# One of eight Q loads split into a half and eight small pieces, in an attention kernel that streams K and V

## The chip, the cores and the metric

The kernel runs on one core of one Trainium2 chip. The metric is the device time of that core in microseconds; lower is better. A core has a matrix engine (TensorE, PE in the profile, with its weight loads as PEld), a vector engine (DVE), a scalar engine (ACT), a general engine (POOL), and a sync engine (SP), which in this kernel issues every DMA. The DMAs of one core are carried out by 16 DMA engines side by side; a transfer adds 16 to its semaphore when it has landed.

## The reference

Grouped-query attention: 16 batches, 32 query heads over 8 key/value heads, 16 query positions, 2048 keys, head size 128, bf16.

```python
B, Hq, Hkv, Sq, Sk, D = 16, 32, 8, 16, 2048, 128
k = jnp.repeat(k, rep, axis=1)          # rep = 4
v = jnp.repeat(v, rep, axis=1)
scores = jnp.einsum("bhqd,bhkd->bhqk", q, k) * D ** -0.5
p = jax.nn.softmax(scores, axis=-1)
return jnp.einsum("bhqk,bhkd->bhqd", p, v)
```

The keys and the values are 64 MiB each; q and the result are 2 MiB each. Every key and value is used by only 64 query rows (4 heads of 16 positions).

## The kernel before, in words

There are 128 groups (batch times key/value head). Two groups make a pair, so that 64 + 64 query rows fill 128 partitions: 64 pairs, `p` from 0 to 63. K is loaded for two pairs at a time (2 MiB, 32 loads, three buffers `Kn`), V for one pair (1 MiB, 64 loads, eight buffers `Vb`; the last one in two parts, `LASTV`), Q for eight pairs (256 KiB, eight loads, numbered `c` = 0 to 7, two buffers `Qn`). The result of a pair is 32 KiB, from twelve buffers.

For a pair, DVE transposes K (`kt`, L562), PE forms the scores into PSUM (`scores`, L406 and L376), DVE copies them out negated and takes the row minimum (`negated`, L573), ACT takes the exponential (L674), PE transposes the probabilities (L414), ACT copies them back (L683), PE multiplies by V (L429, L483, L489), and ACT, or DVE for the last five, scales the result (L697, L701, L655). Q is masked into a block layout by POOL (`lay_part`, L255, four parts for each Q load), transposed by PE (`q_turn`, L392) and copied out by ACT (L664).

The order of the DMAs is written out by hand in one loop of SP (L351 to L367). At step `t` come, if their step is due: a Q load (`load_q`; for `c` of 3 and more at `t = 8c - 13`, so `c` = 7 at `t` = 43), the K load of pairs `t` and `t + 1` (even `t`), a V load (`load_v`), a result's store. SP works them off strictly in turn: each waits for the semaphore that says that its buffer is free, then is issued. A Q load waits for the POOL parts of the Q load two before it (L339).

All eight Q loads have the same form: 128 partitions, and in each partition 8 rows of 128 values, 2 KiB that lie together in HBM. Each adds 16 to the semaphore of its buffer, `sem_q[c % 2]`. POOL waits for it ahead of the first part of that load (L279); its target is 16 times the number of loads so far into that buffer.

Of the kernel before, what the change touches and what calls it, by code (L numbers as in the profile page):

```python
# [18 lines left out]
NQ = 2  # L19
# [7 lines left out]
QAHEAD = 6  # L27
LOOP = (3, 26)
QUNIT = 2
EVBASE = 4  # L30
NMBASE = 6
QTBASE = 1
# [16 lines left out]
def bass_standalone__gqa_softmax__sampling_kernel(  # L49
# [28 lines left out]
    Qn = [sb(f"Qn{i}", [128, 8, 128], BF16) for i in range(NQ)]  # L78
# [17 lines left out]

    def o_done(p):
        return sem_o[p // NOG % (NO // NOG)], 16 * NOG * (p // NO)

    scratch = Sneg[NS - 1]  # L100
    iota_t = scratch[:, 0:128].bitcast(I32)
# [12 lines left out]
    sem_q = [sem(f"sem_q{i}") for i in range(NQ)]  # L114
# [26 lines left out]
    NQP = 4 * NQC  # L141
    assert M0 >= QUNIT and M1 % 2 == 0 and M1 + QAHEAD <= NQP
    bank_used = [None] * NSTAGE

    def pe_op(*op):
        pe_prog.append(op)
# [17 lines left out]
    for p in range(2 * M1):  # L164
# [9 lines left out]
        pe_op("S", p + 2)  # L174
        if m < QUNIT:
            for k in ((4,), (5,), (6, 7), ())[p]:
# [43 lines left out]
    for op in pe_prog:  # L220
# [5 lines left out]
        elif op[1] < max(NP - 8, 2 * M1 - 2):  # L226
            bank, done = op[2], (op[2], EVBASE + op[1] + 1)
        else:
            bank, done = banks % NSTAGE, (op[2], EVBASE + op[1] + 1)
            banks += 1  # L230
# [3 lines left out]
    def stage_ap(op):  # L234
        return ST_ps[:, 512 * stage_of[op]:512 * (stage_of[op] + 1)]

    def copies(n):
        return QUNIT < n <= M1

# [9 lines left out]
    def lay_part(eng, k):  # L249
        c, i = divmod(k, 4)  # L250
        b, x = divmod(i, 2)
        src = q_wide(c)[:, b, 4 * x:4 * (x + 1), :].unsqueeze(2).to_broadcast([128, 4, 4, 64])
        by = mask[:, :].unsqueeze(1).unsqueeze(3).to_broadcast([128, 4, 4, 64])
        region = i if c < 2 else 0
        return eng.tensor_tensor(Q4[:, region, :, :, :], src, by, op=ALU.mult)  # L255

    with nc.Block() as block:

        @block.gpsimd
        def _(gp):  # L260
            gp.iota(iota_m[:, :, :], [[-8, 4], [-32, 4]], base=0, channel_multiplier=1).then_inc(sem_id, 1)
            gp.iota(iota_t[:, :], [[1, 128]], base=0, channel_multiplier=-1).then_inc(sem_id, 1)
            gp.wait_ge(sem_id, 2)
            gp.tensor_scalar(ident4[:, :], iota_t[:, :], 0.0, None, op0=ALU.is_equal).then_inc(sem_id, 1)
            gp.tensor_scalar(lo_m[:, :, :], iota_m[:, :, :], 0.0, None, op0=ALU.is_ge).then_inc(sem_id, 1)
            gp.tensor_scalar(hi_m[:, :, :], iota_m[:, :, :], 8.0, None, op0=ALU.is_lt).then_inc(sem_id, 1)
            gp.wait_ge(sem_id, 5)
            gp.tensor_tensor(lo_m[:, :, :], lo_m[:, :, :], hi_m[:, :, :], op=ALU.mult).then_inc(sem_id, 1)
            for x in range(2):
                gp.wait_ge(sem_id, 6 + x)  # L270
                a = lo_m[:, :, :] if x == 0 else hi_m[:, :, :]
                w = 2 >> x
                dst = hi_m[:, :, 0:2] if x == 0 else mask[:, :].unsqueeze(2)
                gp.tensor_tensor(dst, a[:, :, 0:w], a[:, :, w:2 * w], op=ALU.add).then_inc(sem_id, 1)
            gp.wait_ge(sem_id, 8)
            def part(k):
                c, i = divmod(k, 4)
                if i == 0:
                    gp.wait_ge(sem_q[c % NQ], 16 * (c // NQ + 1))  # L279
                gp.wait_ge(sem_stq, k - 3 if c < 2 else 5 if k == 8 else k)  # L280
                ins = lay_part(gp, k)
                if c < 2:
                    ins.then_inc(sem_qb, 1)
                else:
                    ins.then_inc(sem_q4, 1 + (Q4BASE if k == 8 else 0))

            def copy(n):
                c, i = divmod(n, 4)
                gp.wait_ge(sem_s, 2 * n)
                if i == 0 or n == QUNIT + 1:  # L290
                    gp.wait_ge(sem_qe, 4 * c + 4)
                if n == QUNIT + 1:
                    gp.wait_ge(sem_stq, 8)
                gp.tensor_copy(  # L294
                    QTq[:, :, :, :].rearrange("p b n e -> p b (n e)").bitcast(I32),
                    QT[c % 2][:, :, 256 * i:256 * (i + 1)].bitcast(I32),
                ).then_inc(sem_qt, 1 + (QTBASE if n == QUNIT + 1 else 0))

            for k in range(4, QUNIT + QAHEAD + 1):
                part(k)  # L300
            copy(QUNIT + 1)
            for m in range(QUNIT, M1):
                if m + QAHEAD + 1 < NQP:
                    part(m + QAHEAD + 1)
                if copies(m + 2):
                    copy(m + 2)
            for k in range(M1 + QAHEAD + 1, NQP):
                part(k)

        @block.sync  # L310
        def _(sp):
            def load_k(n):
                s = n % NK
                if n >= NK:
                    sp.wait_ge(sem_kt, 4 * (n - NK) + 4)
                sp.dma_start(Kn[s][:, :], kf[n]).then_inc(sem_k[s], 16)  # L316

            def load_v(p):
                s = p % NV
                if p >= NV:  # L320
                    sp.wait_ge(sem_pv, p - NV + 1)
                if p < NP - 1:
                    dst = Vb[:, s, :, :, :].rearrange("a g j d -> a g (j d)")
                    sp.dma_start(dst, vf[:, 2 * p:2 * p + 2, :]).then_inc(sem_v[s], 16)
                    return
                for x, (lo, hi) in enumerate(LASTV):
                    dst = Vb[:, s, :, lo:hi, :].rearrange("a g j d -> a g (j d)")
                    src = vf[:, 2 * p:2 * p + 2, 128 * lo:128 * hi]
                    sp.dma_start(dst, src).then_inc(sem_vl[x], 16)

            def load_q(c):
                s = c % NQ
                if c >= NQ:
                    if c == 2:
                        sp.wait_ge(sem_qa, 4)
                    elif c == 3:
                        sp.wait_ge(sem_qb, 4)
                    else:
                        sp.wait_ge(sem_q4, Q4BASE + 4 * (c - NQ) - 4)  # L339
                src = qf[1024 * c:1024 * (c + 1), :].rearrange("(a j) d -> a j d", j=8)  # L340
                sp.dma_start(Qn[s][:, :, :], src).then_inc(sem_q[s], 16)

            def store(p):
                s = p % NO
                if p < NP - NLATE:
                    sp.wait_ge(sem_nm, NMBASE + p + 1)
                else:
                    sp.wait_ge(sem_nl, p - (NP - NLATE) + 1)
                sp.dma_start(of[128 * p:128 * (p + 1), :], Osb[s][:, :]).then_inc(o_done(p)[0], 16)  # L349

            for t in range(NP + SLAG + 1):  # L351
                if t == 4:
                    for s in range(NV):
                        sp.sem_inc(sem_v[s], VBASE)
                    sp.sem_inc(sem_nm, NMBASE)
                    sp.sem_inc(sem_exp, EXPBASE)
                for c in range(NQC):
                    if t == (QLOAD[c] if c < len(QLOAD) else 8 * c - QLEAD):
                        load_q(c)
                if t < NP and t % 2 == 0:  # L360
                    load_k(t // 2)
                if 0 <= t - VLAG < VLATE:
                    load_v(t - VLAG)
                if VLATE <= t - VLAG - 1 < NP:
                    load_v(t - VLAG - 1)
                if 0 <= t - SLAG < NP:
                    store(t - SLAG)  # L367
            for g in range(NO // NOG):
                sp.wait_ge(sem_o[g], 16 * NOG * len(range(g, NP // NOG, NO // NOG)))

        @block.tensor
        def _(pe):
# [63 lines left out]
            def emit(op):  # L436
# [30 lines left out]
                elif op[0] == "PV":  # L467
                    p = op[1]
                    pe.wait_ge(sem_ev[1], EVBASE + p + 1)
                    if p < NP - 1:  # L470
# [187 lines left out]
        def _(act):  # L658
            for op in act_prog:
# [19 lines left out]
                elif op[0] == "pe":  # L679
# [5 lines left out]
                        stage_ap(("PT", p, h)), ACT.Copy,  # L685
                    ).then_inc(sem_ev[h], 1 + (EVBASE if p == 0 else 0))
                else:
# [43 lines left out]
```

## Time and profile before

| | us |
|---|---|
| median of 3 runs | 339.18 |
| lowest, highest | 339.04, 339.88 |
| the profiled execution's own time | 338.73 |
| its span, first to last instruction | 336.9 |
| DVE busy | 304.7 (90%) |
| PE busy | 299.8 (89%) |
| ACT busy | 245.9 (73%) |
| POOL busy | 69.7 (21%) |
| time of the data queue's packets, share of 16 engines' span | 100.6% |

The span is what the profile covers; the 1.8 us up to the profiled execution's time lie outside its first and last instruction. All times within the profile are counted from the span's start. The data queue's share is the sum of its packets' times over 16 engines times the span; packets of one engine overlap a little, so it can pass 100%. HBM reads are 136.31 MB and writes 2.10 MB, 411 GB/s over the span. The granted TensorE clock was 0.995 of full speed.

### The profile page before, as it was taken

To read this page: it belongs to the slowest core of one execution; us is meant where nothing else is said; L and a number is where in the kernel's file an instruction comes from. 1 tells how busy PE (TensorE), PEld (TensorE's weight loads), DVE (VectorE), ACT (ScalarE), POOL (GpSimd) and SP (SyncE) were. 2 spreads that over 40 slices of the span, in tenths; PEclk is the share of its full clock that TensorE was granted. 3 is DMA by queue.
4 is the path that set the end of the run, shared out by engine and by line. 5 is a ranking of instruction groups with operands and counts; after the bars stand their busy time and mean duration, and the time that the engine had idled before them with its cause. 6 is when DMAs were issued, how large, how long until landed. Compare 5 with 4: busy or idle time off the path is not lost.

```text
span 336.9 us, 7946 instructions
## 1 busy us (share of the span) xinstructions
PE 299.8 (89%) x3264; PEld 172.9 (51%) x2752; DVE 304.7 (90%) x457; ACT 245.9 (73%) x376; POOL 69.7 (21%) x64
## 2 busy tenths in 40 slices
PE   3466899999999999999998998889898879999885
PEld 3012456655566555665555456455465445555564
DVE  1788999999999999999998999989899999999941
ACT  3124887888888898888876877767867787877873
POOL 2802022221222222222122222022221200000000
PEclk9998999999999999999999999999999999999999
DMA  7999999999999999999999999999999999999996
GB/s 294 443 413 431 414 410 408 418 424 426 420 413 413 423 424 422 417 411 421 426 427 416 410 417 424 425 418 422 409 422 425 430 416 424 418 411 416 413 412 226
DMA packets 32670, 138.60 MB, mean 411 GB/s; under 512 B 10896, under 2 KB 11152, under 8 KB 28560
## 3 DMA queue, kind: packets, MB, share of 16 engines
q1 hardware_dynamic: 32656, 138.42, 100.6%
q8 instruction: 8, 0.13, 0.2%
q14 instruction: 6, 0.05, 0.0%
HBM read 136.31 MB, written 2.10 MB: 411 GB/s over the span
## 4 chain that ended last, share of the span: by engine, by line
DMA 39%; PE 32%; DVE 21%; ACT 3%; issue 2%; SPq 2%; DVEq 0%; ACTq 0%
DMA Kn<-in_k_dram 25%; DMA Vb<-in_v_dram 14%; DVE Sneg L573 11%; DVE KT L562 10%; PE O_ps L429 9%; PE S_ps L406 8%; PE S_ps L376 7%; PE ST_ps L414 6%; PE ST_ps L392 2%; ACT P L674 1%; SPq L349 1%; ACT PT L683 1%; ACT QT L664 0%; PE S_ps L489 0%; SPq L316 0%
## 5 line engine op out<-in xcount | busy, mean ns | idle before, releaser
L562 DVE STREAM_TRANSPOSE KT<-Kn 128x1024 f32<-128x1024 f32 x128 | 151.0, 1219 | 9.0 <-DMA Kn<-in_k_dram 9.0
L573 DVE TENSOR_SCALAR_CACHE_REDUCE Sneg<-S_ps 128x1024 f32<-128x1024 f32 x128 | 150.1, 1207 | 8.5 <-PE S_ps L376 8.4
L674 ACT ACTIVATE P<-Sneg,nbias 128x2048 bf16<-128x2048 f32 x64 | 128.1, 2002 | 31.7 <-DVE nbias L582 15.7
L255 POOL TENSOR_TENSOR Q<-Qn,mask 128x1024 bf16<-128x1024 bf16 x28 | 52.9, 1894 | 135.4 <-PE ST_ps L392 128.9
L429 PE MATMUL O_ps<-Vb,PT 128*64 (+1 forms) x1104 | 68.8, 238 | 11.3 <-DMA Vb<-in_v_dram 10.2
L406 PE MATMUL S_ps<-KT,Q 64*128 64x512 bf16 x384 | 74.8, 386 | 0.0
L376 PE MATMUL S_ps<-KT,Q 64*128 64x512 bf16 x384 | 74.2, 383 | 0.0
L429 PEld LDWEIGHTS O_ps<-Vb,PT 128*64 128x64 bf16 (+1 forms) x1104 | 55.6, 106 | 35.2 <-issue 27.9
L683 ACT ACTIVATE PT<-ST_ps 128x512 f32<-128x512 f32 x128 | 68.8, 590 | 3.0 <-PE ST_ps L414 2.2
L414 PE MATMUL ST_ps<-ident,P 128*128 128x128 f32 x512 | 68.2, 276 | 1.5 <-ACT PT L683 1.2
L414 PEld LDWEIGHTS ST_ps<-ident,P 128*128 128x128 f32 x512 | 56.3, 141 | 5.9 <-ACT P L674 2.2
L697 ACT ACTIVATE O<-O_ps,rrec 64x128 bf16<-64x128 f32 x56 | 20.3, 362 | 38.2 <-PE O_ps L429 30.9
L406 PEld LDWEIGHTS S_ps<-KT,Q 64*128 64x128 bf16 x384 | 18.6, 93 | 49.7 <-issue 38.2
L406 PE MATMUL S_ps<-KT,QT 64*128 64x512 bf16 x128 | 28.2, 423 | 13.5 <-DVE Sneg L573 9.8
L392 PEld LDWEIGHTS ST_ps<-ident,Q 128*128 128x128 f32 x128 | 15.2, 153 | 25.4 <-issue 25.4
L376 PE MATMUL S_ps<-KT,QT 64*128 64x512 bf16 x128 | 28.2, 422 | 0.0
L392 PE MATMUL ST_ps<-ident,Q 128*128 128x128 f32 x128 | 22.2, 306 | 6.6 <-DVE Q L605 5.4
L294 POOL COPY Q<-QT 128x512 int32<-128x512 int32 x24 | 14.6, 610 | 58.8 <-PE S_ps L376 58.8
L664 ACT ACTIVATE QT<-ST_ps 128x512 f32<-128x512 f32 x32 | 19.3, 603 | 9.8 <-PE ST_ps L392 9.8
L406 PEld LDWEIGHTS S_ps<-KT,QT 64*128 64x128 bf16 x128 | 7.7, 99 | 34.1 <-issue 29.5
L701 ACT ACTIVATE O<-O_ps,rrec 128x128 bf16<-128x128 f32 x31 | 11.7, 378 | 2.4 <-PE O_ps L489 2.3
L674 ACT ACTIVATION_READ_ACCUMULATOR P<-Sneg,nbias 128x1 f32 x64 | 12.0, 188 | 0.0
(25 smaller groups left out, 71.6 us busy)
## 6 DMA issues: line engine op xcount, KB each, us to landing
Kn<-in_k_dram SPq DMA_DIRECT2D x32, 2048.0 KB, 18.6
Vb<-in_v_dram SPq DMA_DIRECT2D x63, 1024.0 KB, 16.9
Qn<-in_q_dram SPq DMA_DIRECT2D x8, 256.0 KB, 14.7
out_dram<-O SPq DMA_DIRECT2D x64, 32.0 KB, 16.1
Vb<-in_v_dram SPq DMA_DIRECT2D x1, 768.0 KB, 12.8
Vb<-in_v_dram SPq DMA_DIRECT2D x1, 256.0 KB, 12.5
```

The source lines that it names most:

```text
L255: return eng.tensor_tensor(Q4[:, region, :, :, :], src, by, op=ALU.mult)
L376: return pe.add_instruction(mybir.InstMatmult(name=nc.get_next_instruction_name(), engine=mybir.EngineType.PE, ins=[pe.lower_ap(rhs), pe.l ...
L392: ins = pe.transpose(dst[:, 128 * j:128 * (j + 1)], src[:, j, :], ident4[:, :])
L406: ins = pe.matmul(s_ap, w, x, start=(acc == 0), stop=(acc == 3))
L414: ins = pe.transpose(dst[:, 128 * t:128 * (t + 1)], ptile[:, 128 * x:128 * (x + 1)], ident4[:, :])
L429: return pe.add_instruction(mybir.InstMatmult(name=nc.get_next_instruction_name(), engine=mybir.EngineType.PE, ins=[x, pe.lower_ap(w, for_ ...
L562: dve.transpose(KT[n % NKT][:, :].rearrange("p (t b g e a) -> p e g t b a", t=J // 4, b=2, g=4, e=2)[:, e], Kn[Q % NK][:, :].bitcast(F32). ...
L573: ins = dve.tensor_scalar(Sneg[p % NS][:, 1024 * x:1024 * (x + 1)].rearrange("p (t a m) -> p t a m", t=4, m=8), S_ps[:, 1024 * y:1024 * (y ...
L664: act.activation(QT[c % 2][:, i // 2, :].rearrange("p (a x j) -> p x a j", x=2, j=4)[:, i % 2], stage_ap(("Q", k)).rearrange("p (j a) -> p ...
L674: act.activation(P[p % 2][:, :].bitcast(BF16), Sneg[p % NS][:, :], ACT.Exp, bias=col(nbias, p), scale=-1.0, accum_out=col(rowsum, p),).the ...
L683: act.activation(PT[slot][:, 4 * h:4 * (h + 1), :].rearrange("p t q -> p (t q)"), stage_ap(("PT", p, h)), ACT.Copy,).then_inc(sem_ev[h], 1 ...
L697: ins = act.activation(Osb[p % NO][rows, :], O_ps[rows, 128 * g:128 * (g + 1)], ACT.Copy, scale=col(rrec, p)[rows])
```

## The change

The load of `c` = 7, the last of the eight, is issued as nine transfers in a row: partitions 0 to 63 in one of 128 KiB, then partitions 64 to 71, 72 to 79 and so on up to 127 in eight of 16 KiB. All nine add 16 each to the same semaphore, so that the wait for this load has the target 16 × (1 + 1 + 1 + 9) = 192 where it was 64. The other seven loads, the waits ahead of the issue, the step at which it comes, the bytes and all instructions of PE, DVE, ACT and POOL stay as they are; SP has eight instructions more.

```diff
+QSPLIT = 7
+QROWS = 8
@@
+    def q_pieces(c):
+        if c != QSPLIT:
+            return [(0, 128)]
+        return [(0, 64)] + [(a, a + QROWS) for a in range(64, 128, QROWS)]
+
+    def q_loaded(c):
+        return 16 * sum(len(q_pieces(x)) for x in range(c % NQ, c + 1, NQ))
@@ part (POOL)
-                    gp.wait_ge(sem_q[c % NQ], 16 * (c // NQ + 1))
+                    gp.wait_ge(sem_q[c % NQ], q_loaded(c))
@@ load_q (SP)
-                sp.dma_start(Qn[s][:, :, :], src).then_inc(sem_q[s], 16)
+                for lo, hi in q_pieces(c):
+                    sp.dma_start(Qn[s][lo:hi, :, :], src[lo:hi]).then_inc(sem_q[s], 16)
```

## The prediction

> **What bounds the kernel now.** I read the page's part 2 first, then the stretches around the changed load, its queue (part 3), the chain, and last SP's own line of time.
>
> ```profile
> DVE  1788999999999999999998999989899999999941
> DMA  7999999999999999999999999999999999999996
> GB/s 294 443 413 431 414 410 408 418 424 426 420 413 413 423 424 422 417 411 421 426 427 416 410 417 424 425 418 422 409 422 425 430 416 424 418 411 416 413 412 226
> ...
> q1 hardware_dynamic: 32656, 138.42, 100.6%
> q8 instruction: 8, 0.13, 0.2%
> ...
> DMA 39%; PE 32%; DVE 21%; ACT 3%; issue 2%; SPq 2%; DVEq 0%; ACTq 0%
> ```
>
> The DMA engines are at 90% or more in all slices but the first and the last, at a level rate. DVE is as full to the eye, but the chain (the last line) names DMA first. The table by stretch settles it:
>
> ```profile
> 155.00:205.00 50.00, 46.33 (x503) 26.92 (x422) 47.81 (x71) 38.56 (x60) 12.52 (x10) 1.00 1.02 420
> 205.00:285.00 80.00, 71.48 (x782) 41.03 (x652) 73.95 (x110) 60.94 (x94) 15.01 (x12) 1.00 1.02 420
> ```
>
> The columns are stretch, length, busy time of PE, PEld, DVE, ACT, POOL, clock, DMA share, GB/s. From 205 to 285 us DVE works 73.95 of 80 us, so it idles 6 us; the DMA engines have a share of 1.02, no idle time at all. The bound is the stream of 138 MB, and the end of the run is the end of the last V load: in the chain that load takes 12.82 us to 333.23 us, and only 1.10 us of PE, 0.35 us of DVE and a store come behind it.
>
> So what counts is whether one of the 16 DMA engines gets more to do. They keep their distance: the trace's landing records hold the 16 increments of each load. The K load that landed at 35.0 us has them within 0.56 us; the next one, at 46.2 us, has one engine 1.2 us behind the other 15, after an instruction fetch of 16 KB that began at 41.0 us and took 1.06 us. The spread is 1.70 us at the last Q load (213.9 us), and 1.94 us at the last part of V. A delay of one engine isn't made up, as its queue is never empty. At the end the last increment has three others within 0.1 us, four 0.4 to 0.5 us ahead, eight 1.0 to 1.9 us ahead.
>
> Now the place of the change:
>
> ```profile
> 192.93 5.63 SPq L349 DMA_DIRECT2D out_dram<-O  x1
> 198.60 1.17 SPq L341 DMA_DIRECT2D Qn<-in_q_dram  x1
> 199.82 0.44 SPq L324 DMA_DIRECT2D Vb<-in_v_dram  x1
> 200.30 2.26 SPq L349 DMA_DIRECT2D out_dram<-O  x1
> 202.60 1.91 SPq L316 DMA_DIRECT2D Kn<-in_k_dram  x1
> 204.55 3.37 SPq L324 DMA_DIRECT2D Vb<-in_v_dram  x1
> ```
>
> An issue that nothing holds up takes 0.33 to 0.47 us (the early K and V loads). Those of 1 to 5 us are held up, some by the semaphore of a buffer, many by the queue being full: the Q load's 1.17 us end with no semaphore near. Eight transfers are outstanding then, and it lands 15.3 us after its issue.
>
> **The change part by part.** The sum is made against the profiled execution's 338.73 us (span 336.9 and 1.83 outside it), which is 0.45 us below the median of the runs, 339.18.
>
> *Eight more issues on SP, at about 198.6 us.* Eight by 0.43 us is 3.4 us; if each were held up like the Q load (1.17 us), 9.4 us. Queued behind them are the V load of 199.82, a store, the K load of 202.60 and all later ones; DVE waits for that K, PE for that V. The V load would leave between 203 and 209 us. What was issued ahead of it lands up to 213.9 us, so the DMA engines have 5 us of work left even then, and the K load was held until 204.5 us anyhow. Taken: 0, between 0 and, should that cover go, the 3.4 us.
>
> *POOL's wait.* The load lands at 213.9 us; its first part (the fourth from the last of POOL's masks) starts at 229.66 us, after 6.29 us of waiting for PE. Cost 0 with 15.7 us of cover; past that POOL, then PE's transpose of Q would be late.
>
> *The packets on the DMA engines.* Before: 1024 packets of 2 KB in eight loads, 128 a load, 8 an engine; median 84 ns, 81 to 312 ns. After: the half gives 4 to each of 16 engines, a piece has 8 packets. If they fall on the same eight engines each time, those have 4 + 8 = 12, the other eight 4. So eight engines get 4 × 0.084 = 0.34 us more and eight get 0.34 us less. Were they dealt out evenly it would be 0; were a whole piece on one engine, always the same, 60 × 0.084 = 5.0 us. No row shows a transfer of fewer than 128 partitions; I take the eight, as the row nearest to it, a full load, gives one packet to one row and equal numbers to as many engines as it can.
>
> [...]
>
> *Completion writes.* Eight more on each of these, at a median of 9 ns (packets of 4 bytes): 0.07 us. That they don't stall the engine shows in the stores: one of 32 KB lands 0.16 to 0.20 us behind the V load ahead of it, and its eight packets of 18 ns take 0.14.
>
> *Packets that meet.* The rows of a piece lie side by side, and eight engines write them while the other eight go on with their own. Nothing of before shows the price. From below it is 0 (each packet 84 ns); from above all eight take the slowest 2 KB packet of the trace, 8 × (312 − 84) = 1.82 us. I take each packet shared with one other, twice 84 ns: 0.67 us, nearer to the lower end, where 9 in 10 of those packets are (85 ns or less).
>
> *Sum.* 0.34 + 0.07 + 0.67 = 1.08 us on eight engines. If these were eight drawn from 16, at least one of the four last is among them in 96 of 100 draws, so nothing is deducted. The end moves from 338.73 to 339.8, against the median from 339.18 to **340.3 us**; the bounds are +0.4 (339.6) and +2.2 (341.4).
>
> **The rivals.**
>
> *A: the pieces go one at a time.* For: the slowest packet row, and eight writers on neighbouring rows. Against: the median row, and that the 16 engines stand up to 1.7 us apart, so that they come to a piece at different times. Price: the upper bound, +2.2 us, 341.4 us. [...]
>
> *B: the queue counts transfers, not bytes.* For: SP is held up with 7 to 10 outstanding, early and late. Against: held-up issues end in the middle of K loads too, so packets seem to be counted. If transfers count, nine pieces fill the queue, and the V load leaves when the work ahead is gone. The first load of the run, into an empty queue, needs 2.7 us to land; less some 1 us of the pieces' own work that is a hole of 1.7 us in all engines, with the 1.1 from above +2.8: 342.0 us. It decides if the limit is 10 or fewer.
>
> *C, to the other side: the relieved engines are the last.* If the four last engines are all among the eight that lose 4 packets, the end comes 0.34 us earlier, 338.8 us, until the loaded eight, 0.4 to 0.5 us ahead, catch up. It decides only with no meeting of packets. Against: 4 in 100 draws; but whatever makes engines late may single out one half of them.
>
> *D: instruction fetches fall otherwise.* The eight of 16 KB take 0.93 to 1.11 us each on one engine. With eight more instructions on SP they may hit others: from −1.1 us (338.1), where all of the last four are spared one, to +1.0.
>
> *E: no net shift,* the pieces being dealt out evenly: 339.2 us.
>
> **How the numbers follow.** No change is told from one of up to 0.3%, which is 1.0 us: 338.16 to 340.20. The main case 0.52 (0.30 of it above 340.2, as the bounds reach from 339.6 to 341.4 and the value taken is just over the line), A 0.14, B 0.10, C 0.10, E 0.06, D 0.08 (half faster). Slower: 0.30 + 0.14 + 0.10 = 0.54; faster 0.04 from D and 0.03 from C together with it, 0.07; the rest 0.39. Predicted 340.3. The range reaches from C's 338.8 to a little over B's 342.0, 342.2, and leaves out D's early half and the starved end of SP.
>
> **What would show it.** Right: nine Q rows on SP, 0.4 to 1.2 us each; the K and V landings behind them spread wider by 1 us and staying so; DMA share level at 1.02. A: the pieces' packets near 0.3 us. B: a dip in the DMA row at about 212 us and issue times that jump. C: a spread that shrinks. I am wrong if the spread after the pieces doesn't change, if the pieces are on all 16 engines, or if SP's 3.4 us open a hole.

## The result, and the profile after

The changed kernel takes 340.40 us (median of 10 runs, 339.96 to 341.54), the kernel before in the same batch 339.21 us (10 runs, 338.65 to 339.88). The ratio is 1.0038, with a 95% interval of 1.0027 to 1.0049: slower by 1.2 us. The profiled execution took 340.31 us, 1.58 more than the one before.

The rows of the page of the changed kernel that answer to those of before (shares and rates in 40 slices of the span, the data queue, the chain by engine):

```profile
span 338.5 us, 7954 instructions
...
DMA  7999999999999999999999999999999999999996
GB/s 295 445 412 428 422 404 411 418 424 431 412 414 415 422 424 425 418 407 418 423 430 418 415 411 420 377 416 419 412 421 425 427 420 422 418 409 417 413 413 205
...
q1 hardware_dynamic: 32720, 138.42, 100.5%
q8 instruction: 8, 0.13, 0.2%
...
DVE 50%; DMA 34%; PE 9%; issue 3%; ACT 2%; SPq 2%; DVEq 0%; ACTq 0%
```

The DMA row is the same as before, digit by digit, but in the 26th slice, 212 to 220 us, the rate falls from 425 to 377 GB/s. The data queue has 64 packets more and the same bytes. The chain's shares have moved from DMA to DVE; that is no new bound. Where two engines are nearly as full, the chain can go back along either, and its end is what it was. The chain from 320 us on (start, duration, what):

```profile
320.87 1.18 SPq L360
322.05 0.04 issue
322.10 12.73 DMA Vb<-in_v_dram
334.82 0.14 issue
334.96 1.10 PE S_ps L500 x32
336.06 0.02 issue
336.08 0.35 DVE O L666
```

The last V load again sets the end, it lands 1.59 us later (334.82 for 333.23 us), and what comes behind it costs what it did. SP's own line of time (start, duration, instruction):

```profile
192.88 5.63 SPq L360 DMA_DIRECT2D out_dram<-O  x1
198.55 4.10 SPq L352 DMA_DIRECT2D Qn<-in_q_dram  x9
202.70 0.40 SPq L334 DMA_DIRECT2D Vb<-in_v_dram  x1
203.15 0.99 SPq L360 DMA_DIRECT2D out_dram<-O  x1
204.19 3.37 SPq L326 DMA_DIRECT2D Kn<-in_k_dram  x1
207.60 1.17 SPq L334 DMA_DIRECT2D Vb<-in_v_dram  x1
```

Nine issues take 4.10 us in place of 1.17, and the V load behind them leaves at 202.70 instead of 199.82 us. Did that starve the engines? The same two stretches as before (stretch, length, busy time of PE, PEld, DVE, ACT, POOL, clock, DMA share, GB/s), and behind them three short ones around the landing of the Q load:

```profile
155.00:205.00 50.00, 46.30 (x504) 26.91 (x422) 47.79 (x71) 38.60 (x60) 12.53 (x10) 1.00 1.02 419
205.00:285.00 80.00, 71.79 (x749) 40.93 (x619) 72.48 (x109) 59.67 (x93) 15.04 (x12) 0.98 1.02 413
208.00:211.00 3.00, 3.00 (x50) 2.13 (x46) 2.65 (x6) 2.46 (x7) 1.90 (x1) 1.00 0.95 389
211.00:215.00 4.00, 2.20 (x20) 1.00 (x13) 4.00 (x5) 2.54 (x4) 0.61 (x1) 1.00 1.05 296
215.00:219.00 4.00, 4.00 (x36) 2.22 (x27) 2.86 (x6) 2.70 (x4) 0.00 (x0) 1.00 1.06 436
```

The same three short stretches of the kernel before:

```profile
208.00:211.00 3.00, 3.00 (x50) 2.18 (x46) 2.65 (x6) 2.45 (x7) 1.89 (x1) 1.00 0.92 378
211.00:215.00 4.00, 2.91 (x28) 1.59 (x19) 4.00 (x5) 2.59 (x4) 0.61 (x1) 1.00 1.09 430
215.00:219.00 4.00, 4.00 (x44) 2.13 (x35) 3.57 (x6) 3.35 (x6) 0.17 (x1) 1.00 1.00 425
```

No idle time shows: from 211 to 215 us the DMA share is 1.05 (1.09 before). But the DMA engines move 296 GB/s in place of 430. Against before that is (430 − 296) × 4 − (389 − 378) × 3 − (436 − 425) × 4 = 459 KB less, at 413 GB/s 1.1 us. The loss is all there. The K load that lands ahead, at 210.7 us, comes within 0.04 us of its old time; the next one 1.1 us later (222.6 for 221.5). In the mean of a load's 16 landings the delay stays between 1.0 and 1.2 us from there to the end.

The trace's packet records say what the engines did with the time. Around the last Q load I add up by how much every packet took longer than its kind does undisturbed (84 ns for a packet of Q, 159 ns for one of 4 KB, of V), and divide by 16 engines: 0.08 us before, 1.27 us after. The packets of Q grow from 84 to 105 ns in the mean, 168 at most. The packets of V beside them grow from 160 to 235 ns in the mean, 518 at most, and of 20.3 us of engine time lost they hold 16.6, Q's own 2.7. So the transfers that were cut lost little themselves; they slow down their neighbours.

### The profile page after: what moved, and what is told of

It is laid out like the page before. It is cut to its first block, busy times and chain, and to the rows that moved or that the text cites. A ratio compares the mean times of both kernels' runs of the same rounds, so it can differ in the third digit from the quotient of the medians.

```text
span 338.5 us, 7954 instructions
## 1 busy us (share of the span) xinstructions
PE 301.3 (89%) x3264; PEld 173.8 (51%) x2752; DVE 304.4 (90%) x457; ACT 246.1 (73%) x376; POOL 69.8 (21%) x64
## 4 chain that ended last, share of the span: by engine, by line
DVE 50%; DMA 34%; PE 9%; issue 3%; ACT 2%; SPq 2%; DVEq 0%; ACTq 0%
DVE Sneg L584 26%; DMA Kn<-in_k_dram 25%; DVE KT L573 23%; DMA Vb<-in_v_dram 9%; PE S_ps L417 3%; PE S_ps L387 2%; PE O_ps L440 2%; PE ST_ps L425 1%; SPq L360 1%; ACT P L685 1%; ACT PT L694 1%; DVE rrec L580 0%; PE ST_ps L403 0%; PE S_ps L500 0%; SPq L334 0%
## 5 line engine op out<-in xcount | busy, mean ns | idle before, releaser
L440 PE MATMUL O_ps<-Vb,PT 128*64 (+1 forms) x1104 | 70.5, 240 | 11.1 <-DMA Vb<-in_v_dram 9.9
L440 PEld LDWEIGHTS O_ps<-Vb,PT 128*64 128x64 bf16 (+1 forms) x1104 | 56.4, 106 | 35.6 <-issue 29.1
L708 ACT ACTIVATE O<-O_ps,rrec 64x128 bf16<-64x128 f32 x56 | 20.3, 363 | 39.3 <-PE O_ps L440 32.2
```

The costliest lines, as they stand in the source:

```text
L440: return pe.add_instruction(mybir.InstMatmult(name=nc.get_next_instruction_name(), engine=mybir.EngineType.PE, ins=[x, pe.lower_ap(w, for_ ...
L708: ins = act.activation(Osb[p % NO][rows, :], O_ps[rows, 128 * g:128 * (g + 1)], ACT.Copy, scale=col(rrec, p)[rows])
```

## The experiments

A single cut costs only 1.2 us, so most kernels cut five Q loads, `c` = 3 to 7 (a 5 at the end of the label); three cut only `c` = 7 (a 1). All share this edit of the kernel before; a piece is (first partition, step, count), and only the list and `QSPLIT` differ:

```diff
+    def q_pieces(c):
+        return LIST if c in QSPLIT else [(0, 1, 128)]
+
+    def q_loaded(c):
+        return 16 * sum(len(q_pieces(x)) for x in range(c % NQ, c + 1, NQ))
-                    gp.wait_ge(sem_q[c % NQ], 16 * (c // NQ + 1))
+                    gp.wait_ge(sem_q[c % NQ], q_loaded(c))
-                sp.dma_start(Qn[s][:, :, :], src).then_inc(sem_q[s], 16)
+                for a, step, n in q_pieces(c):
+                    rows = slice(a, a + step * (n - 1) + 1, step)
+                    sp.dma_start(Qn[s][rows, :, :], src[rows]).then_inc(sem_q[s], 16)
```

For all of them I also compare, against the profile of before, the mean of the 16 landings of the last V part. That mean tells what all engines lost; the last of the 16 adds what single engines lost. Only one execution of each kernel was profiled, and the executions of a kernel with five cut loads lie up to 3.6 us apart (`strU5`).

**The whole change five times** (`after5`): does the cost repeat?

```diff
+LIST = [(0, 1, 64)] + [(a, 1, 8) for a in range(64, 128, 8)]
```

> The split of the changed kernel made on five Q loads (c = 3 to 7) instead of one, to see its price five times over. Theory M (packets meet: eight engines write into partitions that other engines are writing at the same time, so packets of both get longer and the rate drops): five dips in the DMA rate, +1.2 us each, about 345.2 us against 339.2. Rival U (uneven shares alone: eight engines get four packets more each time, others four fewer): 5 x 0.41 = +2.0 us, 341.2, no dips. Rival Q (nine queue entries or eight more issues on SP): +6 us as M, but idle DMA engines at the dips.

Measured: 348.96 us (before 339.27), ratio 1.0294 (1.0267 to 1.0320), +9.7 us. It repeats and more: theory M had 345.2. The mean landing is 6.67 us later, 1.33 per load, near the 1.19 us of the single change. The rest is distance between the engines: the 16 landings of the last V part, 1.94 us apart before, are 6.0 us apart.

**Two halves, no pieces** (`half5`): meant to give all 16 engines equal shares.

```diff
+LIST = [(0, 1, 64), (64, 1, 64)]
```

> The same five Q loads as two transfers of 64 partitions each, without small pieces. All 16 engines get 4 + 4 = 8 packets as before. Rival U: 0, 339.2 us. Rival Q: one more entry a load, 0 to +0.7 us. [...]

Measured: 344.47 us, ratio 1.0145 (1.0122 to 1.0168), +5.2 us, more than any theory had expected: theory M had 340.2 to 342.2, at +0.2 to +0.6 us a load, an estimate of the author's that rests on which partitions an engine writes, and no run shows that. The mean landing is 6.39 us later, nearly as much as with the pieces, but the 16 landings are only 2.7 us apart. (The profiled execution of `half5`, 345.70 us, is its slowest, that of `after5`, 348.16, among its faster ones; by the medians two halves bring 5.2 of 9.7 us.) So at least half of the cost doesn't need the pieces: the cut into two halves brings it.

**Other pieces.** `strL5` has the upper half in one transfer and the lower in pieces of eight partitions four apart. `strU5` has the order of the change, with the upper half in such strided pieces, where a piece of the change has eight neighbouring partitions.

```diff
+LIST = [(64, 1, 64)] + [(32 * b + m, 4, 8) for b in range(2) for m in range(4)]   # strL5
+LIST = [(0, 1, 64)] + [(64 + 32 * b + m, 4, 8) for b in range(2) for m in range(4)]   # strU5
```

> The same five Q loads: partitions 64 to 127 in one transfer, 0 to 63 in eight pieces of eight partitions that are four apart (0, 4, 8 to 28; 1, 5 to 29; and so on), so the number of transfers and the shares of the engines are those of the changed kernel. [...] Left are the uneven share, +0.41, and the half, +0.2 to +0.6: +0.6 to +1.0 a load, 342.2 to 344.2 us, 2 KB packets of the pieces back at 84 ns. Rivals U and Q: as in the five contiguous splits, whatever these give.

> The same five Q loads: partitions 0 to 63 in one transfer, 64 to 127 in eight pieces of eight partitions that are four apart. Shares, transfers and partitions are those of the changed kernel, only the partitions that go together differ. [...] Rivals U and Q: the same as the five contiguous splits.

Measured: `strL5` 346.81 us, 1.0222 (1.0194 to 1.0249); `strU5` 349.78 us, 1.0334 (1.0294 to 1.0374). Both lie above the ranges that theory M gave, 342.2 to 344.2 and 342.7 to 344.7 us; for these, too, the author had supposed which partitions an engine writes. And `strU5` isn't below `after5`: pieces of partitions four apart are not faster than those of eight neighbours, 349.8 against 349.0 us. So how closely a piece's partitions lie is not the price. But which half goes in pieces makes 3.0 us.

**The halves alone.** One half of the five loads is left out, the other is loaded in strided pieces (`own5` the lower, `vis5` the upper) or in one transfer (`low64x5` the lower).

```diff
+LIST = [(32 * b + m, 4, 8) for b in range(2) for m in range(4)]   # own5, own1
+LIST = [(64 + 32 * b + m, 4, 8) for b in range(2) for m in range(4)]   # vis5
+LIST = [(0, 1, 64)]   # low64x5
```

> Five Q loads (c = 3 to 7) bring partitions 0 to 63 only, in eight pieces of eight partitions four apart; partitions 64 to 127 are left out and keep older rows. [...] Rival S (small or partial transfers lengthen packets wherever they go): +0.7 us a load and more, 342.5 us and up.

> The same with the other half: partitions 64 to 127 in eight pieces of eight partitions four apart, 0 to 63 left out. Only the number 64 is added to each destination and its source row; engines, counts and bytes are those of the run with partitions 0 to 63. [...] Rivals S and Q: the same time as with partitions 0 to 63.

> Five Q loads bring partitions 0 to 63 only, in one transfer of 64 partitions that runs on all 16 engines, 4 packets each; partitions 64 to 127 are left out. Without meeting the end would come 5 x 0.34 = 1.7 us earlier, 337.5 us. [...]

Theory M had 339.3 to 339.8 us for `own5`, 342.5 to 345 for `vis5` and 339 to 341 for `low64x5`, on the same supposition, by which packets meet in `vis5` and `low64x5` and not in `own5`.

Measured, against 338.98 us: `own5` 340.91, 1.0045 (1.0026 to 1.0064); `vis5` 344.11, 1.0153 (1.0132 to 1.0173); `low64x5` 341.56, 1.0068 (1.0048 to 1.0088), 0.6 us above its range. The rates in 40 slices, first of `own5`:

```profile
GB/s 293 441 415 421 383 398 412 417 426 428 404 419 419 421 421 415 421 416 416 421 415 423 417 416 418 415 419 422 416 419 422 422 423 414 422 419 407 412 389 116
```

of `vis5`:

```profile
GB/s 300 439 414 418 425 380 408 415 424 425 376 419 415 420 423 372 421 412 418 422 364 424 414 418 416 366 417 426 413 422 419 423 420 420 418 420 408 415 405 145
```

and of `low64x5`:

```profile
GB/s 300 441 413 424 420 382 407 419 425 426 388 410 414 421 426 392 419 410 420 424 384 422 416 411 423 397 417 412 413 420 424 431 413 428 416 409 416 413 413 180
```

The five loads land in slices 6, 11, 16, 21 and 26. `vis5` dips in all five, to 364 to 380; `low64x5` in all five, to 382 to 397. In `own5` the last three show no dip, and its packets of Q take 84 ns as in the whole load (93 in the first of the five), those of `vis5` 104 to 115. Eight pieces of eight partitions cost the stream next to nothing in the lower half and a microsecond in the upper. So it isn't the pieces' size, nor their number.

What differs is where the pieces go. The semaphore updates in the trace show eight a piece from DMA engines and one more, so the eight packets of a piece go out on eight engines. By theory M a piece to the upper half meets packets of V from other engines, and a piece to the lower half doesn't. Packets of Q at 104 to 115 ns in `vis5` and at 84 ns in `own5` fit that, but it stays the author's reading: the trace names neither the engine nor the partitions of a packet.

`own5` misses its expectation by over 1 us. Slices 5 and 6 are low, and in the trace the gap begins in a K load at 39 us, ahead of any piece's packets: 16 KB packets of K, 611 ns in the median before, take up to 2.0 us, and that load's mean landing is 1.01 us late. SP issues the eight pieces of the first cut load at that time, from 38.0 to 43.7 us; `vis5`, where that goes from 35.6 to 41.1 us, has no such gap. Whether the issues play a part stays open.

**Destination or source?** The strided pieces of `own5` and `vis5` differ in the rows of HBM too. `srcU5` writes to the lower half what belongs to the upper; `dstU5` the reverse.

```diff
+LIST = [(32 * b + m, 4, 8) for b in range(2) for m in range(4)]   # srcU5, reads src[rows + 64]
+LIST = [(64 + 32 * b + m, 4, 8) for b in range(2) for m in range(4)]   # dstU5, reads src[rows - 64]
```

> As the five-fold run with pieces into partitions 0 to 63 (the upper half left out), but the rows are read from where those of partitions 64 to 127 lie, 128 KB on in HBM, so that the partitions get the wrong rows. If the destination decides: 2 KB packets at 84 ns and 0.2 us of lengthened packets a load, 340 to 341.5 us. If the source decides: 105 ns, 1.0 us or more, 344 us.

> The mirror: pieces into partitions 64 to 127 (the lower half left out) with the rows of 0 to 63. If the destination decides: dips as with the proper rows, 2 KB packets at 104 to 107 ns, 1.0 us or more of lengthened packets a load, 343.5 to 345 us. If the source decides: 84 ns, 340 to 341.5 us.

Measured, against 339.24 us: `srcU5` 340.81, 1.0038 (1.0022 to 1.0053); `dstU5` 345.58, 1.0183 (1.0133 to 1.0233, from two runs, 344.38 and 346.78), by the median 0.6 us above its range. Rates of `srcU5`:

```profile
GB/s 299 447 407 426 396 387 403 423 421 430 404 413 422 423 426 413 421 413 417 423 415 430 410 415 419 416 422 421 413 420 416 426 420 418 425 413 409 415 405 129
```

and of `dstU5`:

```profile
GB/s 299 441 412 420 392 388 409 418 423 427 379 419 416 423 422 374 417 412 418 423 357 425 413 417 419 367 425 414 416 419 422 425 418 422 426 407 413 414 410 144
```

The dips go with the destination: 379, 374, 357 and 367 in the last four loads of `dstU5`, 404, 413, 415 and 416 in `srcU5`. Packets of Q take 84 ns in `srcU5`, 100 to 111 in `dstU5`. So the loss lies on the side of SBUF, not of HBM. Both kernels are low in slices 5 and 6, near the first cut load, as `own5` was; the K load ahead of it is 0.34 and 0.46 us late.

**A cut that leaves the partitions whole** (`free5`): two transfers to 128 partitions each, cut along the row.

```diff
+        return [0, 4] if c in QSPLIT else [0]
+                for j in q_pieces(c):
+                    w = 8 // len(q_pieces(c))
+                    sp.dma_start(Qn[s][:, j:j + w, :], src[:, j:j + w, :]).then_inc(sem_q[s], 16)
```

> Five Q loads (c = 3 to 7) in two transfers each, cut along the row and not along the partitions: all 128 partitions get values 0 to 511 of their 1024, then the rest. As many transfers as the two halves of 64 partitions (+5.2 us there), packets of 1 KB (16 an engine, 46 ns, +0.07 us a load). Theory M: every engine keeps its partitions, no meeting: +0.1 to +0.6 us in all, 339.2 to 339.8 us, no dips. If two transfers as such cost (rival Q): 344 us.

Measured: 339.31 us (10 runs) against 339.24, ratio 1.0008 (0.9992 to 1.0024): nothing, though each of the five loads is two transfers of packets half as long. A second issue and smaller packets are free here; two transfers cost 5.2 us only if they cut the partitions. The stretch around the last Q load (columns as above):

```profile
211.00:215.00 4.00, 2.98 (x28) 1.40 (x19) 3.96 (x5) 2.97 (x4) 0.61 (x1) 1.00 1.05 404
```

**One load alone**: `half1` is `half5`, `own1` is `own5`, for `c` = 7 only.

> Only the load c = 7, in two transfers of 64 partitions, no small pieces. Shares of the engines even. By the five-fold run (+5.2 us, mean landing +1.3 a load) this alone brings +1.0 us, 340.3 us, as much as the whole change: then the small pieces' meeting takes the place of the second half's and their uneven share adds at most 0.4 us. If the eight pieces are what costs, 339.3 to 339.5 us.

> [...] Theory M: no dip, 2 KB packets at 84 ns, end within 0.3 us of before, 338.9 to 339.5 us. The five-fold run's +1.9 us would give +0.4.

Measured: `half1` 340.32 us against 338.98, ratio 1.0050 (1.0030 to 1.0070); `own1` 339.34 against 339.24, 1.0008 (0.9994 to 1.0021). The stretch of the loss (columns as above), first in `half1`:

```profile
211.00:215.00 4.00, 1.79 (x18) 0.60 (x9) 4.00 (x5) 2.57 (x4) 0.61 (x1) 1.00 1.06 276
```

and in `own1`:

```profile
211.00:215.00 4.00, 2.97 (x29) 1.68 (x20) 4.00 (x5) 2.56 (x4) 0.61 (x1) 1.00 1.07 407
```

Two halves without a piece bring the rate from 430 to 276 GB/s and cost 1.3 us, as much as the whole change; the eight pieces of `own1` leave it at 407, where `free5` has 404, and the time shows no cost.

**The runs side by side.** What a cut load costs: how far the mean landing shifts from the loads just ahead of it to those just behind it, plus, where half of the load is left out, the 0.34 us (64 packets of 84 ns over 16 engines) that the engines are spared in the mean. The table has the mean over `c` = 4 to 7, or `c` = 7 alone where only that is cut; `c` = 3 is left out for the gap ahead of it in three kernels. Beside it, how the load is written.

| | partitions written, and how | cost per load, us |
|---|---|---|
| `free5` | all 128, in two transfers cut along the row | 0.06 |
| `own5`, `srcU5` | lower half in eight pieces | 0.16, 0.16 |
| `own1` | lower half in eight pieces | 0.16 |
| `low64x5` | lower half in one | 0.75 |
| `strL5` | upper half in one, lower in eight pieces | 1.11 |
| `vis5`, `dstU5` | upper half in eight pieces | 1.10, 1.07 |
| `half5`, `half1` | each half in one | 1.33, 1.35 |
| `after5`, the change | lower half in one, upper in eight pieces of neighbours | 1.38, 1.10 |
| `strU5` | lower half in one, upper in eight pieces four apart | 1.66 |

For example `vis5`, whose shift goes from 0.37 to 3.39 us: 3.02 / 4 + 0.34 = 1.10. Whole partitions cost next to nothing; of the cuts across them, eight pieces are the cheapest way in the lower half (0.16, in one transfer 0.75) and cost 1.1 in the upper. The halves don't simply add up: `low64x5` and `vis5` together, 1.85, are above `strU5`, 1.66, which writes the same pieces.

**What stays open.** Why `own5`, `srcU5` and `own1` have 0.16 us with Q's packets at 84 ns in the first two; there too the neighbours' packets are longer, in `own1` seven of V over 200 ns, 392 at most. Why the neighbours lose more than the load's own packets take: in `low64x5` 64 packets of 84 ns are 5.4 us of engine time, and 0.70 to 0.97 us on each of 16 engines, 11 to 16 us, are lost. And which engine writes which partitions, in a transfer of 8, 64 or 128: no record shows it. No kernel has other engines write the small pieces, so the pieces alone don't exclude that the upper half is dear for them whoever writes it; `low64x5`, which loses in the lower half, speaks against that as the whole account.

## Why the prediction was right

**The time.** 340.3 us predicted, 340.40 measured, and the bound named, the stream of the DMA engines, is the one that decided. The sum in the middle was right in size but not in its make.

**SP's eight issues at nothing: right.** They took 2.9 us more, within the 3.4 us worked out, and the V load left at 202.70 us, just short of the 203 to 209 us named. The cover held, as no stretch shows idle DMA engines. `free5` shows the same for five extra issues, one a load.

**POOL's wait at nothing: right.** The load's last landing moved from 213.9 to 215.8 us, with its first use at 232.45 us.

**Eight engines a piece, +0.34 and −0.34 us, 0.07 of completion writes: right in kind, smaller when measured, and seen only when repeated.** Each piece has eight updates from DMA engines and one more, and 16 are left for the half (88 in all). That the eight are the same each time no record names; what speaks for it is how far the landings part. By the terms, the two sets of engines should part by 0.34 + 0.34 + 0.07 = 0.75 us a load. In the V load that lands behind the last cut load (at 224.0 us before) the 16 landings are 2.85 us apart in `half5`, 5.49 in `after5`, 5.30 in `strL5` and 4.88 in `strU5`: for each load with pieces 0.53, 0.49 and 0.41 us more than with two halves. (At the end it is 2.7, 6.0, 6.4 and 5.4 us.) In the single change, the landings that were 1.70 us apart are 1.8 apart afterwards: the engines stand that far apart anyway, so a part of the 0.75 goes into gaps between them.

**"Packets that meet" at 0.67 us: the step that failed.** Longer packets are there, but the step named the wrong packets, the wrong transfers and the wrong engines. It counted the pieces' own packets, twice 84 ns, on eight engines. Measured, a packet of Q goes from 84 to 105 ns, a quarter of what was taken, and the packets of V from 160 to 235; the 16 engines lose 1.19 us in the mean (1.27 − 0.08). And the transfer of half the partitions, which the prediction gave nothing, costs too: 0.75 us a load in `low64x5`, and two of them, without a piece, 1.3 us in `half1`. The right account is about 1.2 us on all engines, to which the uneven shares add a few tenths at most at the end of a single change. The predicted 1.08 came out near the measured 1.19 us by luck: an overrated term for eight engines stood in for a missing one for all.

**The rivals.** A, the pieces one at a time with packets of 0.3 us: no, in the change they take 168 ns at most, and pieces of partitions four apart were no faster (`strU5` 349.78 us, `after5` 348.96). B, transfers filling the queue: no, the DMA share never fell, and at 209.3 us 17 transfers are outstanding (11 at most around the Q load before), where B needed a limit of 10 or fewer. C, the relieved engines the last: no sign, since all engines lose. D, fetches that fall otherwise: at most in part. The first three began at 41.6, 47.2 and 52.3 us, before at 41.1, 47.2 and 52.4. But in the profiled execution the last landing's delay goes from 1.21 us (the V load of 318.2 us before) to 1.82 (that of 320.8), with the mean delay unchanged two loads later, and a fetch of 1.0 us begins at 320.46 us (319.34 before). So some 0.4 of the 1.59 us at the end may be a fetch that fell on a later engine. E, no net shift: excluded by the interval of the ratio.

**What was to show it.** Nine Q rows on SP, yes, but the pieces took 0.28 to 0.52 us each, for 0.4 to 1.2 forecast; DMA share level, yes. The landings "spread wider by 1 us": no, behind the pieces they moved together by 1.1, and in the last V part they are 2.47 us apart for 1.94. That was named as a sign that the prediction is wrong, and it is the sign that half of the account was.

## What to carry to other kernels

In a stream that fills all DMA engines, cut a side load along its rows and leave its 128 partitions whole: `free5` cost nothing that could be measured for five loads, the same loads cut into two halves of the partitions 5.2 us. A DMA share at 1.0 doesn't say that nothing is lost (in the change 296 GB/s at 1.05); look at GB/s beside it, and at the neighbours' packet times, not at the cut transfer's. Where one engine's delay or share is in question, repeat the change: the uneven shares that a single load hid (landings 1.8 us apart behind it) came out at five (5.49 us in `after5`).

## What the runs showed of the hardware that was not expected

- Two transfers of 64 partitions each cost 1.3 us beside a full stream (`half1`), 4 us at 276 in place of 430 GB/s with a DMA share of 1.06 (1.09 before).
- The cost goes with the partitions written, not with the rows read: +1.6 us for `srcU5`, +6.3 us for `dstU5`, which swap the two.
- Most of the time is lost in packets of other transfers, in the change 16.6 of 20.3 us of engine time: those of V, 160 to 235 ns in the mean, 518 at most, beside Q packets of 105 ns.
- The delay isn't made up: in the change the mean landing stays 1.0 to 1.2 us late to the end. Nor is the distance between engines: five uneven loads left the 16 landings of the last V part 6.0 us apart (`after5`), 1.94 before.
